# Score pieces moved from the middle to the end of a step's second product

## The chip, the cores and the metric

One core of one Trainium2 chip runs the whole program in one launch. The metric is device time in microseconds (us), the median of several runs. TensorE (PE) multiplies, with its weight loads listed apart (PEld); VectorE (DVE), ScalarE (ACT) and GpSimd (POOL) work on tiles; SyncE (SP) issues most DMAs.

## The reference, cut to what matters

Three layers follow one another: block-causal attention, a token-mixing layer with a two-layer perceptron, and a gated layer.

```python
scores = q @ k.T / 8, block-causal mask with blocks of 64   # 8 batches x 8 heads, 576 tokens, 64 wide
x      = softmax(scores) @ v                                # heads side by side: [8, 576, 512]
u      = x + (x.T @ U @ V).T                                # mixing over the tokens, rank 32
y      = u + relu(u @ w_ch1) @ w_ch2                        # 512 -> 2048 -> 512
out    = (sigmoid(causal_conv5(y)) * (y @ w_val)) @ w_out
```

## The kernel before, in words

**Perceptron.** The 4608 tokens are cut into 9 groups of 512 (`groups`). Each group is worked in 16 steps, one per 128 hidden units. A step has two products of 12 matmuls of 512 columns each. The first (`emit_h1`, L1000, matmuls at L987) sums a bank `h` of PSUM; ACT then writes `hh = relu(h)` (L1015) and DVE writes the rest `hl = max(h,0) - hh` (L1016), since every float32 product is made of three products of high and low parts. The second (`emit_o`, L1023, matmuls at L1036) adds `hh` and `hl` of the step before (`LAG = 1`) into four banks `acc` that are held over the group. So PE's row of work is h(s), o(s-1), h(s+1), o(s), and so on.

**Gaps.** PE runs in the order in which the program is written (`manual_schedule`). The order on the other engines is made by a scheduler when the program is built. Attention for later batches is a generator (`attention`, `tick`, L860) that is resumed in the gaps of the perceptron: `gap(0)` after six matmuls of the first product, `gap(1)` behind it, once ACT's and DVE's reads of the bank are issued, `gap(2)` after six matmuls of the second product, `gap(3)` behind it. These numbers are the kinds of a gap. A group has 64 gaps.

**The timetable.** From the tenth pair of heads on (`PAIR0`), each piece of attention waits in `until` (L844) for its gap. `begun[g]` is the count of gaps when group g began; pair i of the group gets its piece `what` at the first gap whose count is at least `begun[g] + POS0 + period * i + PLACES[..][what]`. The period is 12 gaps (three steps) in group 1, which takes five pairs, and 16 gaps (four steps) in groups 2 to 6, which take four, four, four, four and one. Pieces that put matmuls on PE also refuse a gap that another such piece has used. Only this line has a condition on the kind of gap:

```python
yield from until(n, f"S{i}", (2, 3))     # L876, i = 0 or 2
emit_s_piece(n // 2, i)
emit_s_piece(n // 2, i + 1)
```

**The pieces of a pair.** S0 and S1 together, then S2 and S3 together: scores of two heads (L420, two banks of PSUM a piece, one per head, copied out by ACT at L425). In between and behind: corner masks (POOL), block maxima (DVE L618), transposes of the next q and k (L398, L399), the running maximum of a head and its subtraction (DVE L651 to L671, `x` in the table for the odd head), the exponentials (ACT L687, in two halves of 832 and 768 columns) and sums (POOL L694, L696, DVE L703). V is probability times value (L729, L739, copied by ACT L741, divided by DVE L746 to L749 and POOL L750), T transposes (L789, L797), G and H mix over tokens (L805 with ACT L807, DVE L808; L828 with DVE L830). H of the batch's last pair ends the batch, and H pieces that had to wait for a free `u` buffer are put in at the group's end (`flush_later`).

**PSUM.** While attention runs, four banks are `acc` and four (`ps_p`, tag `a`) are shared by h, S, V, T, G and H in turn: a new piece takes the bank that was taken four allocations ago and waits until its reader, ACT or DVE, is done. S0, S1 take four in a row: the fourth is that of the piece before S0.

Of the kernel before, what the change touches and what calls it, by code (L numbers as in the profile page):

```python
# [22 lines left out]
def attn_moe_gate_kernel(ctx: ExitStack, tc: tile.TileContext, q, k, v, U, V, w1, w2, wval, convw, wout, out):  # L23
    nc = tc.nc
    B, H, S, D = q.shape
# [58 lines left out]
    FLUSH = 4  # L84
    PAIR0 = (NQ + EARLY) // 2
    PAIR1 = 3 * NP + 3
    POS0 = 6
    PLACES = (
        (12, {"S0": 0, "m0": 2, "S2": 4, "H0": 5, "H1": 6, "T0": 7, "T1": 8, "V": 9, "m1": 10, "G": 11, "x": 11}),
        (16, {"S0": 0, "m0": 2, "S2": 4, "H0": 5, "H1": 6, "T0": 7, "T1": 8, "V": 9, "m1": 11, "G": 14, "x": 15}),  # L90
# [254 lines left out]
    def load_v(n):  # L345
        if not 0 <= n < NH:
            return
        vv = v[n // H, n % H]
        t = vpart(n)
        sp.dma_start(out=t[:, 0:NK - 1, :], in_=vv[0:S - D, :].rearrange("(i p) d -> p i d", p=P))  # L350
        sp.dma_start(out=t[D:P, NK - 1, :], in_=vv[S - D:S, :])
# [56 lines left out]
    def emit_s_piece(pn, i):  # L408

        heads = (2 * pn, 2 * pn + 1)  # L410
        tq, tk = qkt[pn]
        if i == 0:
            for n in heads:
                stt[n] = [spare(("za", "zb")[h], w) if n % 3 == 1 else s_p.tile([P, w], F32, tag=f"s{h}", name=f"s{h}") for h, w in enumerate(sw)]
        ps = [psum["a"].tile([P, 512], F32, tag="a", name="pS") for _ in own]
        o = 0
        for j, a0, a1 in pieces[i]:
            w = a1 - a0
            for t, me in zip(ps, own):
                pe.matmul(t[:, o:o + w], tk[me, kslice(j)], tq[me, a0:a1], start=True, stop=True)  # L420
            o += w
        j, a0, a1 = pieces[i][0]
        d = soff[j] + a0 - q0[j]
        for n, t in zip(heads, ps):
            act.copy(stt[n][half_of[j]][:, d:d + o], t[:, 0:o])  # L425
# [172 lines left out]
    def emit_corners(n):  # L598
        for h, js in enumerate(((3, 0), (1, 2))):
            c0, c1 = (soff[j] // D for j in js)  # L600
            v_ = stt[n][h].rearrange("p (c w) -> p c w", w=D)
            pool.memset(v_[D:P, c0:c1 + 1:c1 - c0, :], MASKED)
        pool.memset(sv(n, NK - 1)[0:D], MASKED)
# [11 lines left out]
    def emit_max_a(n):  # L615
        r = tiny_p.tile([P, sum(nblk)], F32, tag="rb", name="rb")
        for half, (o, w) in enumerate(((0, nblk[0]), (nblk[0], nblk[1]))):
            x = vec.tensor_reduce(  # L618
                r[:, o:o + w],
                stt[n][half].rearrange("p (b a) -> p b a", a=BL),  # L620
                axis=AX.X,
                op=ALU.max,
                apply_transpose=True,
            )
        noted(1, x)
        mxt[n] = r

    def emit_max_b(n):

        t = mxt.pop(n)  # L630
        r = tiny_p.tile([P, NB32], F32, tag="r0", name="r0")

        def join(out, i, j):
            a, b = t[:, rblk[i]], t[:, rblk[j]]
            skip = (q0[j] - q0[i]) // BL
            if out is None:
                vec.tensor_tensor(a[:, skip:], a[:, skip:], b, op=ALU.max)
            else:
                vec.tensor_tensor(out[:, skip:], a[:, skip:], b, op=ALU.max)
                vec.tensor_copy(out[:, 0:skip], a[:, 0:skip])  # L640

        join(None, 1, 2)
        join(None, 3, 4)
        join(None, 1, 3)
        join(r, 0, 1)
        mxt[n] = r
# [21 lines left out]
    def emit_sub(n, half):  # L668
        mb = mbt[n]
        for j in parts[half]:  # L670
            noted(3, vec.tensor_tensor(sv(n, j), sv(n, j), mb[:, q0[j]:], op=ALU.subtract))  # L671
# [6 lines left out]
    def emit_exp(n):  # L678
        pn, a = divmod(n, 2)
        src = stt.pop(n)  # L680
        if a:
            dst = src
        else:
            e = late["e"] if pn % 2 and "e" in late else e_p
            dst = [e.tile([P, w], F32, tag=f"e{h}", name="e") for h, w in enumerate(sw)]
        for s, t in zip(src, dst):
            act.activation(t, s, AF.Exp, scale=scale)  # L687
        est[n] = dst
# [10 lines left out]
    def emit_sum_b(n):  # L699
        m = sums[n]  # L700
        r = tiny_p.tile([P, NB32], F32, tag="rs", bufs=3, name="rs")
        for o, t in ((slice(0, P // BL), ev(n, 0)[:, 0:P]), (slice(P // BL, NB32), m)):
            vec.tensor_reduce(r[:, o], t.rearrange("p (b a) -> p b a", a=BL), axis=AX.X, op=ALU.add, apply_transpose=True)  # L703
        sums[n] = r
# [12 lines left out]
    def emit_pv(pn, c):  # L717
        heads = (2 * pn, 2 * pn + 1)
        if c == 0:
            xts[pn] = (late["x"] if heads[0] >= 3 * H and pn % (NP + 2) == 0 else x_p).tile([P, S], F32, tag="xt", name="xt")  # L720
        xt = xts[pn]
        last[0] = (own[0], xt[own[0]][0:1, 0:1])
        ps = ps_p.tile([P, 512], F32, tag="a", name="pPV")
        c0, c1 = vbanks[c]
        js = [j for j in range(NK) if q0[j] < c1]
        for j in js:
            a0 = max(c0, q0[j])
            for n, me in zip(heads, own):
                pe.matmul(  # L729
                    ps[me, a0 - c0:c1 - c0],  # L730
                    vpart(n)[:, j, :],
                    est[n][half_of[j]][:, soff[j] + a0 - q0[j]:soff[j] + c1 - q0[j]],
                    start=j == 0,
                    stop=j == js[-1],
                )
        if c:
            f = ps[:, c1 - c0:c1 - c0 + NB32]
            for n, me in zip(heads, own):
                pe.matmul(f[me], quad, sums.pop(n), start=True, stop=True)  # L739
        with tc.high_priority():  # L740
            act.copy(xt[:, c0:c1], ps[:, 0:c1 - c0])  # L741
        if c:
            for n in heads:
                est.pop(n)
            r = tiny_p.tile([P, NB32], F32, tag="r0", name="r0")
            vec.tensor_scalar(r, f, 1e-9, None, op0=ALU.add)  # L746
            vec.reciprocal(r, r)
            rb = rot("t")
            vec.transpose(rb.rearrange("p (j a) -> p j a", a=32), r.rearrange("p (j o) -> p j o", o=1).to_broadcast([P, NB32, 32]))  # L749
            pool.tensor_tensor(xt, xt, rb, op=ALU.mult)  # L750
# [93 lines left out]
    def until(n, what, kinds=None):  # L844

        p = n // 2
        if p < PAIR0:
            return
        g, i = (1, p - PAIR0) if p < PAIR1 else (2 + (p - PAIR1) // NP, (p - PAIR1) % NP)
        period, place = PLACES[g > 1]  # L850
        busy = what[0] in "SHTVG"
        while at_gap["kind"] != FLUSH:
            c = at_gap["count"]
            if g in begun and c >= begun[g] + POS0 + period * i + place[what] and (kinds is None or at_gap["kind"] in kinds) and not (busy and at_gap["used"] == c):
                break
            yield WAITS
        if busy:
            at_gap["used"] = at_gap["count"]

    def tick(n, mixed, last=B * NP):  # L860


        e = n - DEPTH
        new, half = n < NH, n % 2
        pn = n // 2 - 1
        old = NQ <= 2 * pn < NH

        if old and not half:
            load_v(n - 2)
            load_v(n - 1)  # L870
        for i in range(4):
            if new and not half:
                if n < 2 * PAIR0:
                    emit_s_piece(n // 2, i)
                elif i % 2 == 0:
                    yield from until(n, f"S{i}", (2, 3))  # L876
                    emit_s_piece(n // 2, i)
                    emit_s_piece(n // 2, i + 1)
            if old and half and i == 0:
                yield from until(n, "V")  # L880
                emit_pv(pn, 0)
                emit_pv(pn, 1)
            if i == (0 if half else 3) and new:
                emit_corners(n)
                emit_max_a(n)
            if i == (2 if half or n < 2 * PAIR0 else 1) and NQ <= n - 1 < NH:
                yield from until(n, f"m{half}")
                emit_sum_b(n - 1)
            yield
        if new:  # L890
            emit_max_b(n)
            if half:
                prep_t((n + 1) // 2)
        yield from mixing(2 * e, mixed, last)
        if half:
            yield from until(n, "x")
        if new:
            for _ in emit_max_c(n):
                pass
            emit_sub(n, 0)  # L900
            emit_sub(n, 1)
            emit_exp(n)
            emit_sum_a(n)
        yield from mixing(2 * e + 1, mixed, last)
# [323 lines left out]
    for s in range(NS + LAG):  # L1228
        g, f = divmod(s, NF)
# [89 lines left out]
```

## Time and profile before

| | us |
|---|---|
| median of 3 runs | 1389.25 (1387.07 to 1389.58) |
| the profiled execution | 1385.46 |
| its span, first to last instruction | 1383.7 |
| PE busy | 1333.4 (96%) |
| DVE busy | 986.6 (71%) |
| ACT busy | 552.6 (40%) |
| POOL busy | 445.1 (32%) |
| mean granted clock of TensorE | 0.991 of full speed |

A matmul that follows another is listed with its whole length, 0.39 us for 512 columns, though one begins every 0.23 us. So the listed idle time of PE is less than what a wait costs: that is read from the start of the work behind the wait. Starts are counted from the start of the span.

### The profile page before, as it was taken

Reading aid. Unit: us, or ns where it says so; the run is one execution under the profiler, and the core shown is the slowest. Engines: PE = TensorE matmul, PEld = TensorE weight load, DVE = VectorE, ACT = ScalarE, POOL = GpSimd, SP = SyncE. Lnnn points to the kernel's source line nnn. Section 1 sums busy time; section 2 is a strip of 40 time slices with the busy share of each in tenths; the row PEclk is TensorE's granted clock in tenths of the full one; section 3 lists DMA queues with packets and bytes.
Section 4 is the critical chain, followed back from the end, with each engine's and each line's share of the span. In section 5 each row is a group of like instructions: output and inputs, shape, how many; then the busy total and the mean of one; then the engine's idle time right before and its main releaser. Section 6 shows DMA issues by size and latency. Waiting matters only on the chain.

```text
span 1383.7 us, 20054 instructions
## 1 busy us (share of the span) xinstructions
PE 1333.4 (96%) x6840; PEld 1029.5 (74%) x6840; DVE 986.6 (71%) x2085; ACT 552.6 (40%) x1210; POOL 445.1 (32%) x648
## 2 busy tenths in 40 slices
PE   6889889999999999999999999999999999999999
PEld 4667665777677777777777777778878888788887
DVE  5986789788878778777877877772235164699981
ACT  5785544333343334334433433432223122434432
POOL 3443334423343224334322422441132100624210
PEclk9999998999999999999999999999999999999999
DMA  6667785644364347435443644332375632332311
GB/s 109 159 179 209 230 263 170 140 95 115 78 135 107 93 113 155 111 92 142 104 99 96 155 105 111 102 103 88 116 206 167 154 128 99 77 107 77 107 60 62
DMA packets 257936, 173.60 MB, mean 125 GB/s; under 512 B 202149, under 2 KB 222885, under 8 KB 257834
## 3 DMA queue, kind: packets, MB, share of 16 engines
q1 hardware_dynamic: 250282, 162.58, 42.5%
q0 software_dynamic: 5184, 9.44, 4.5%
q8 instruction: 54, 0.88, 0.3%
q10 hardware_dynamic: 2368, 0.30, 0.2%
q14 instruction: 48, 0.39, 0.1%
HBM read 135.57 MB, written 36.70 MB: 125 GB/s over the span
## 4 chain that ended last, share of the span: by engine, by line
PE 59%; DVE 24%; ACT 7%; DMA 5%; issue 3%; SPq 1%; POOL 0%; ACTq 0%; DVEq 0%; POOLq 0%
PE acc L1036 18%; PE h L987 18%; PE o L1150 7%; PE val L1126 7%; PE pS L420 4%; DMA raw<-in_moe_w_ch_dram 3%; DVE hl L1016 2%; DVE mb L664 2%; PE pPV L729 2%; DVE s L671 2%; DVE r L657 2%; ACT e L687 1%; DVE wa L133 1%; DVE g L105 1%; ACT s L687 1%
## 5 line engine op out<-in xcount | busy, mean ns | idle before, releaser
L1036 PE MATMUL acc<-hh,w 128*128 128x512 f32 x1152 | 404.3, 404 | 1.6 <-DMA w<-w_s 1.6
L1036 PEld LDWEIGHTS acc<-hh,w 128*128 128x128 f32 x1152 | 218.2, 189 | 72.1 <-issue 23.4
L987 PE MATMUL h<-uh,w1hi 128*128 128x512 f32 x576 | 233.1, 405 | 1.2 <-DVE xt L830 1.0
L1036 PE MATMUL acc<-hl,w 128*128 128x512 f32 x576 | 226.7, 394 | 0.2 <-DVE hl L1016 0.2
L987 PE MATMUL h<-uh,w1lo 128*128 128x512 f32 x576 | 226.0, 392 | 0.0
L987 PE MATMUL h<-ul,w1hi 128*128 128x512 f32 x576 | 225.6, 392 | 0.0
L1016 DVE SCALAR_TENSOR_TENSOR hl<-h,hh 128x512 fp32r<-128x512 f32 x144 | 98.6, 685 | 141.3 <-ACT hh L1015 139.7
L1015 ACT ACTIVATE hh<-h 128x512 fp32r<-128x512 f32 x144 | 85.9, 597 | 242.2 <-PE h L987 241.8
L987 PEld LDWEIGHTS h<-uh,w1hi 128*128 128x128 f32 x576 | 108.8, 189 | 27.6 <-issue 1.8
L987 PEld LDWEIGHTS h<-uh,w1lo 128*128 128x128 f32 x576 | 108.7, 189 | 23.7
L1036 PEld LDWEIGHTS acc<-hl,w 128*128 128x128 f32 x576 | 109.5, 190 | 19.8 <-DVE hl L1016 0.5
L987 PEld LDWEIGHTS h<-ul,w1hi 128*128 128x128 f32 x576 | 109.0, 189 | 20.1 <-issue 0.4
L1108 DVE SCALAR_TENSOR_TENSOR gt<-yb,cw,gt 128x516 f32<-128x516 f32 (+1 forms) x144 | 115.2, 830 | 1.4
L420 PE MATMUL pS<-tq,tk 64*128 64x320 f32 (+4 forms) x576 | 99.0, 420 | 13.1 <-DVE hl L1016 10.2
L105 POOL TENSOR_TENSOR yl<-yb,yh 128x512 fp32r<-128x512 f32 (+7 forms) x64 | 66.8, 1077 | 102.7 <-ACT yh L99 102.6
L105 POOL TENSOR_TENSOR ul<-xt,uh 128x512 fp32r<-128x512 f32 (+7 forms) x64 | 60.2, 948 | 112.7 <-ACT uh L99 112.6
L420 PEld LDWEIGHTS pS<-tq,tk 64*128 64x128 f32 x576 | 52.2, 187 | 51.3 <-issue 24.6
L425 ACT COPY s<-pS 128x320 f32<-128x320 f32 (+2 forms) x128 | 59.6, 501 | 36.5 <-PE pS L420 36.5
L671 DVE TENSOR_TENSOR s<-s,mb 128x64 f32<-128x64 f32 (+4 forms) x160 | 70.6, 507 | 0.5
L694 POOL TENSOR_TENSOR m<-e 128x448 f32<-128x448 f32 x24 | 31.0, 1293 | 122.5 <-ACT e L687 117.7
L729 PE MATMUL pPV<-e,vstk 128*64 128x192 f32 (+4 forms) x384 | 70.2, 336 | 0.1
L729 PEld LDWEIGHTS pPV<-e,vstk 128*64 128x64 f32 x384 | 46.8, 137 | 24.5 <-issue 12.6
(180 smaller groups left out, 2502.9 us busy)
## 6 DMA issues: line engine op xcount, KB each, us to landing
w<-w_s SPq DMA_DIRECT2D x144, 512.0 KB, 3.5
rawq<-in_q_dram SPq DMA_DIRECT2D x128, 72.0 KB, 3.0
out_dram<-ot SPq DMA_DIRECT2D x35, 256.0 KB, 2.0
rawk<-in_k_dram SPq DMA_DIRECT2D x124, 72.0 KB, 2.9
vstk<-in_v_dram SPq DMA_DIRECT2D x68, 128.0 KB, 2.9
raw<-in_moe_w_ch_dram SPq DMA_DIRECT2D x64, 128.0 KB, 2.4
raw<-in_moe_w_ch_dram SPq DMA_DIRECT2D x16, 512.0 KB, 3.9
w_s<-wo SPq DMA_DIRECT2D x16, 512.0 KB, 4.3
```

The lines of the kernel that those rows point to most:

```text
L105: eng.tensor_tensor(o, i, f32(h), op=ALU.subtract)
L420: pe.matmul(t[:, o:o + w], tk[me, kslice(j)], tq[me, a0:a1], start=True, stop=True)
L425: act.copy(stt[n][half_of[j]][:, d:d + o], t[:, 0:o])
L671: noted(3, vec.tensor_tensor(sv(n, j), sv(n, j), mb[:, q0[j]:], op=ALU.subtract))
L729: pe.matmul(ps[me, a0 - c0:c1 - c0], vpart(n)[:, j, :], est[n][half_of[j]][:, soff[j] + a0 - q0[j]:soff[j] + c1 - q0[j]], start=j == 0, st ...
L987: pe.matmul(ps[:, 0:n], w[:, d, fs], x[:, d, 0:n], start=(d == 0 and i == 0), stop=(d == ND - 1 and i == 2))
L1015: act.activation(hh[:, 0:n], ps[:, 0:n], AF.Relu)
L1016: latest[0] = vec.scalar_tensor_tensor(hl[:, 0:n], ps[:, 0:n], 0.0, f32(hh[:, 0:n]), op0=ALU.max, op1=ALU.subtract)
L1036: pe.matmul(acc[d][:, 0:n], w[:, wi, ds], x[:, 0:n], start=(f == 0 and i == 0), stop=(f == NF - 1 and i == 2))
L1108: vec.scalar_tensor_tensor(gt[d][:, 0:gw], y[:, d, j:j + gw], cw[:, d, j:j + 1], gt[d][:, 0:gw], op0=ALU.mult, op1=ALU.add)
L1126: pe.matmul(ps[:, 0:n], w[:, d, es], x[:, d, 0:n], start=(i == 0), stop=(i == 3 * ND - 1))
L1150: pe.matmul(ps[:m, cs], x[:, e, a:a + m], w[:, e, cs], start=(i == 0), stop=(i == 3 * ND - 1))
```

## The change

`POS0`, the first gap of a group's first pair, goes from 6 to 8, and the score pieces take gaps of kind 3 alone, the end of the second product, instead of 2 or 3. Nothing else is changed; the instructions are the same.

```diff
-    POS0 = 6
+    POS0 = 8
...
-                    yield from until(n, f"S{i}", (2, 3))
+                    yield from until(n, f"S{i}", (3,))
```

PE, the second pair of group 4 (`acc` is the second product, `h` the first). Before:

```order
L1036 MATMUL acc_6870<-hh,w_7109 128x512
L1036 MATMUL acc_6870<-hl,w_7109 128x512
L1036 MATMUL acc_6870<-hh,w_7109 128x512
L420 MATMUL pS<-tq,tk 128x64 x2
L420 MATMUL pS<-tq,tk 128x192 x2
L420 MATMUL pS<-tq,tk 128x256 x2
L420 MATMUL pS<-tq,tk 128x320 x2
L1036 MATMUL acc_6871<-hh,w_7109 128x512
L1036 MATMUL acc_6871<-hl,w_7109 128x512
```

and with the change:

```order
L1036 MATMUL acc_6847<-hh,w_7086 128x512
L1036 MATMUL acc_6847<-hl,w_7086 128x512
L1036 MATMUL acc_6847<-hh,w_7086 128x512
L420 MATMUL pS<-tq,tk 128x64 x2
L420 MATMUL pS<-tq,tk 128x192 x2
L420 MATMUL pS<-tq,tk 128x256 x2
L420 MATMUL pS<-tq,tk 128x320 x2
L987 MATMUL h_7211<-uh,w1hi 128x512
L987 MATMUL h_7211<-ul,w1hi 128x512
```

S0 and S1 stood with six matmuls of the second product behind them, which need none of the four banks; now a first product stands there, which needs one. S2 and S3 move in the same way. T, V, G and H move by one or two gaps.

PE, the end of group 3 (H of the batch's last pair, and H pieces that had waited). Before:

```order
L987 MATMUL h_6621<-uh,w1hi 128x512
L987 MATMUL h_6621<-ul,w1hi 128x512
L987 MATMUL h_6621<-uh,w1lo 128x512
L828 MATMUL pH<-vst,g 128x320 x2
L1036 MATMUL acc_5603<-hh,w_6577 128x512
```

and with the change:

```order
L987 MATMUL h_6615<-uh,w1hi 128x512
L987 MATMUL h_6615<-ul,w1hi 128x512
L987 MATMUL h_6615<-uh,w1lo 128x512
L828 MATMUL pH<-vst,g 128x320 x3
L1036 MATMUL acc_5578<-hh,w_6577 128x512
```

Three H pieces now stand in one gap behind a first product, where two did; the ends of groups 1, 2, 4, 5 and 6 read alike with other widths. Between the last S2 of a group and the V that the next group begins with stood 60 matmuls of the two products, and now 54.

ACT, the first pair of group 4. Before:

```order
L807 COPY t<-pG 128x128
L99 CAST g<-t 128x128
L425 COPY za<-pS 128x512
L425 COPY s_6881<-pS 128x512
L425 COPY za<-pS 128x320
L687 ACTIVATE s_6533<-s_6533 128x832
L425 COPY s_6881<-pS 128x320
L687 ACTIVATE s_6534<-s_6534 128x768
```

and with the change:

```order
L807 COPY t<-pG 128x128
L99 CAST g<-t 128x128
L687 ACTIVATE s_6539<-s_6539 128x832
L425 COPY za<-pS 128x512
L425 COPY s_6887<-pS 128x512
L687 ACTIVATE s_6540<-s_6540 128x768
L425 COPY za<-pS 128x320
L425 COPY s_6887<-pS 128x320
```

The exponential of the odd head of the pair before now stands ahead of the first copy of S0. It is so at the first pair of groups 2 to 6. In group 1 it stands there in the third, fourth and fifth pair, before the change and with it.

## Rows read from the trace of the kernel before

**Rows 1.** Waits of PE over the whole span: total us, times, longest.
```profile
PE pS L420 <- DVE hl L1016: 10.2, 16, 2.1
```
**Rows 2.** Timeline of PE, S0 and S1 without a wait (start, us, engine, line).
```profile
658.87 1.79 PE L420 MATMUL pS<-tq,tk 64*128 64x64 f32 x16
660.59 0.50 PE L1036 MATMUL acc<-hh,w 128*128 128x512 f32 x1
```
**Rows 3.** Timeline of PE, S0 and S1 with a wait.
```profile
750.93 1.78 PE L420 MATMUL pS<-tq,tk 64*128 64x64 f32 x14
753.01 0.80 PE L420 MATMUL pS<-tq,tk 64*128 64x320 f32 x2 [0.30 <-DVE hl L1016]
753.74 0.50 PE L1036 MATMUL acc<-hh,w 128*128 128x512 f32 x1
```
**Rows 4.** Timeline of PE, S2 and S3 of the same pair.
```profile
759.41 1.56 PE L420 MATMUL pS<-tq,tk 64*128 64x448 f32 x8
760.90 0.50 PE L1036 MATMUL acc<-hh,w 128*128 128x512 f32 x1
```
**Rows 5.** Timeline of DVE and ACT around that wait.
```profile
752.26 0.69 DVE L1016 SCALAR_TENSOR_TENSOR hl<-h,hh 128x512 fp32r<-128x512 f32 x1
...
749.03 0.90 ACT L687 ACTIVATE s<-s 128x832 f32<-128x832 f32 x1 [4.75 <-DVE s L671]
...
751.10 0.59 ACT L1015 ACTIVATE hh<-h 128x512 fp32r<-128x512 f32 x1
752.21 0.59 ACT L425 COPY za<-pS 128x512 f32<-128x512 f32 x1 [0.52 <-PE pS L420]
...
760.46 0.53 ACT L425 COPY zb<-pS 128x448 f32<-128x448 f32 x1 [1.65 <-PE pS L420]
```
**Rows 6.** Stretches from an S2 to a later S2 (us, engines' busy us, clock, DMA).
```profile
274.61:387.63 113.02, 106.58 (x572) 78.11 (x571) 92.97 (x220) 42.26 (x87) 36.47 (x63) 0.97 0.39 93
387.63:418.19 30.56, 30.56 (x172) 23.60 (x171) 23.43 (x60) 14.59 (x31) 14.18 (x22) 1.00 0.68 152
...
883.25:914.35 31.10, 30.96 (x173) 23.85 (x172) 25.10 (x60) 15.35 (x31) 15.70 (x22) 1.00 0.58 144
418.19:511.81 93.62, 92.39 (x502) 70.25 (x501) 73.94 (x170) 34.14 (x69) 28.74 (x51) 1.00 0.40 102
...
790.12:883.25 93.13, 92.27 (x503) 70.15 (x502) 72.28 (x170) 33.45 (x69) 27.50 (x51) 1.00 0.41 99
```
**Rows 7.** Timeline of PE, DVE and ACT from group 3's end to group 4's first S0.
```profile
635.60 1.56 PE L420 MATMUL pS<-tq,tk 64*128 64x448 f32 x8
...
638.60 1.80 DVE L618 TRANSPOSE_TENSOR_REDUCE rb<-s 128x24 f32<-128x768 f32 x2
...
641.80 0.49 DVE L830 TENSOR_TENSOR xt<-pH,xt 128x320 f32<-128x320 f32 x1 [0.62 <-PE pH L828]
...
655.96 0.18 DVE L746 TENSOR_SCALAR r<-pPV 128x18 f32<-128x18 f32 x1 [0.55 <-ACT xt L741]
...
662.22 0.90 ACT L687 ACTIVATE s<-s 128x832 f32<-128x832 f32 x1 [0.66 <-DVE s L671]
```
**Rows 8.** Timeline of ACT and PE in group 1, fourth pair.
```profile
352.70 0.90 ACT L687 ACTIVATE za<-za 128x832 f32<-128x832 f32 x1 [3.74 <-DVE za L671]
...
358.45 2.29 PE L420 MATMUL pS<-tq,tk 64*128 64x448 f32 x8
360.67 0.50 PE L1036 MATMUL acc<-hh,w 128*128 128x512 f32 x1
```
**Rows 9.** Stretches in group 1 around waits (columns as in Rows 6; clock third from last).
```profile
297.00:300.00 3.00, 3.00 (x9) 2.34 (x9) 2.17 (x5) 0.00 (x0) 2.64 (x8) 0.57 0.00 0
320.00:324.00 4.00, 2.55 (x18) 1.62 (x17) 3.87 (x9) 0.80 (x2) 2.13 (x3) 1.00 0.00 0
382.00:385.00 3.00, 3.00 (x8) 2.43 (x8) 1.63 (x4) 1.81 (x4) 2.31 (x6) 0.51 0.51 175
```

## The prediction

> **What bounds the kernel now.** The list of waits names one thing in the stretch that the change touches: matmuls of score pieces wait for DVE's `hl`, 16 times, 10.2 us of listed idle time [rows 1]. The timeline shows what such a wait costs. Without one, the work behind S0 and S1 begins 660.59 - 658.87 = 1.72 us after S0 [rows 2]. With one that is listed as 0.30 it begins 753.74 - 750.93 = 2.81 us after it [rows 3]: 1.09 us, 0.79 more than listed. At 0.79 more for each, the 16 waits cost 10.2 + 12.6 = 22.8 us: twelve in groups 2 to 5 (all pairs but a group's first; 12 x 1.09 = 13.1) and four in group 1 (9.7). The wait is one for a bank. S0 and S1 take four banks in a row, and the fourth is that of the first product before them. Its `hl` ends at 752.95, and S1 goes on at 753.01, 0.06 later [rows 3, 5]. `hl` is late because ACT writes `hh` at 751.10, behind the exponentials that begin at 749.03 after 4.75 us of waiting for DVE's subtraction [rows 5]. So the loop that sets the period of 31.1 us (four stretches of three periods, 93.62 to 93.13, 373.1 in all [rows 6]) runs from S2 through DVE's long chain (maxima, subtraction), ACT's exponential and `hl` back to S1, and through 24 products to the next S2: 759.41 - 753.74 = 5.67 [rows 3, 4]. PE alone would need 1.09 less.
>
> **Inside a group (groups 2 to 5).** The change removes this wait: with six more products ahead of S0, `hl` of 752.95 would come before S1 needs it. It adds another: the first product that now follows S1 takes the bank of S0's first head, which ACT's copy frees. That copy runs from 1.28 to 1.87 us after S0's start (752.21 + 0.59 - 750.93 [rows 3, 5]); with the 0.06 the product begins at 1.93, not 1.72: 0.21 lost. Behind S2 and S3 the copy ends at 760.46 + 0.53 - 759.41 = 1.58, so 1.64 for 1.49 [rows 4, 5]: 0.15 lost. These waits were covered by six products of the second product, which need no bank; that cover is gone. I take 0.36 a pair, since the copies start as soon as PE is through. The bounds are 0 (a copy of 0.59 hidden) and 0.9 (an exponential of 0.90 [rows 5] in front of it). Sum: 12 x (0.36 - 1.09) = **-8.8**.
>
> **From group to group.** From the last S2 of one group to the first S2 of the next there are five stretches, 30.56 to 31.10, mean 30.7 [rows 6], with no wait for `hl`. Here the change adds two.
>
> First, three H pieces in one gap. They take three banks, and the third is that of the first product that has just ended. Counted from S2 at 635.60 [rows 7]: the product starts at 1.64, has 12 matmuls (2.73) and one H piece (0.15) in it, and ends near 4.6. DVE is through with the maxima at 638.60 + 1.80, that is 4.80, then has three additions of about 0.45 (0.49 listed [rows 7], 0.4 from start to start), then `hl`, 0.69 [rows 5]: 6.9. So the third H goes at 6.95 for 4.9: 2.05 lost. Before, the second product stood between.
>
> Second, the exponential of 832 columns that now stands ahead of S0's first copy on ACT. It hung on DVE's chain, which at a group's start hangs on V: DVE's step behind V begins at 655.96 (20.36 after S2), the exponential at 662.22, 6.26 later [rows 7]. V has 54 matmuls ahead instead of 60, which is 6 x 0.23 = 1.36 earlier, but is pushed by 0.15 and 2.05: 0.84 later, so 21.2. The exponential starts at 27.46 and ends at 28.36; the copy ends about 0.5 later, since ACT begins a row some 0.1 before the last one ends: 28.86. The first product follows at 28.92, the next S2 5.67 later at 34.6. Against 30.7 that is 3.9 a stretch. Were the copy on time, S0 at 25.4 and the product at 27.4 would give 33.0, 2.35 lost. I take 3.9, because each piece of it has its row; the bounds are 0.4 (the copies alone) and 4.7 (DVE's chain another 0.8 longer, as much as the rest of POOL's and DVE's rows here differ). Sum: 5 x 3.9 = **+19.5**.
>
> **Group 1.** Four intervals, 113.0 us [rows 6]. In its third to fifth pair the exponential stands ahead of the copy already, at 352.70 in the fourth [rows 8], but six products covered it. Now 352.70 + 0.90 + 0.5 + 0.06 + 5.67 = 359.8 would be the next S2, not 358.45 [rows 8]: 1.4 later. In exchange S2 and S3 lose their own wait (360.67 - 358.45 = 2.22, against 1.49: 0.73 [rows 4, 8]), and DVE's chain starts 0.7 earlier. That is +0.7 three times. The second pair, with the longest wait (2.1 listed, so 2.9), keeps its first copy ahead of the exponential and gains about 3. Sum: +2.1 - 3.1 = **-1.0**, with 3 either way.
>
> **The end.** Group 6 ends with three H pieces too, when DVE has less to do: `hh` 0.59, `hl` 0.69 [rows 5] and the steps between, 1.6; with the last S2's 0.15 it is **+1.7**. The DMAs keep their bytes; on SP's queue the weights of the second product now stand ahead of the q and k loads of their step instead of between them, so they come no later. m0, m1 and x make no PE work, and only place DVE's.
>
> **The sum.** -8.8 + 19.5 - 1.0 + 1.7 = +11.4. Against the profiled execution's 1385.46 that is 1396.9. The runs' median is 3.8 higher, so the forecast is 1389.25 + 11.4 = **1400.6 us**. A difference under 0.2% (2.8 us) is what a measurement of this kernel can't tell from none.
>
> **The rivals.**
>
> *Faster: the group starts are not late.* If DVE's chain at a group's start is through 1.6 us earlier than I have it (the exponential at 25.9 or before), S0's copy is on time; and if `hl` comes before DVE's additions, the third H waits 0.5. Then a stretch between groups loses 0.9, the pairs gain as above, group 1 gains 3: -8.8 + 4.5 - 3 + 0.7 = -6.6, 1382.6. For it: the 12 waits inside the groups do go, and DVE is busy only 23.43 of 30.56 us there [rows 6], so it has slack. Against it: ACT and DVE work in the order that the program has, and that order has the exponential ahead of the copy and the third addition behind `hl`. It decides at a loss of 1.6 a stretch, where 5 x 1.6 meets the gain.
>
> *No change.* Only one of the two comes, 2.35 a stretch, with group 1 gaining 3: -8.8 + 11.8 - 3 + 1.7 = +1.7, 1391.
>
> *Slower still: the clock.* Two of group 1's waits are followed by a clock of 0.57 and 0.51 of full (near the lower level of 1.2 GHz) for about 3 us [rows 9], which costs some 1.5 us each; a wait as long at 320 to 324 left it at 1.00. The change makes new waits of 1.5 to 4 us: one and a half to two at each of six group ends or starts, and three in group 1. If every one dropped the clock, 13 drops for two would cost 11 x 1.5 = 16 more: 1417. The Trainium skill ("TensorE: Matmul & The Clock Gate", section "What's actually happening") says that half clock is the default state and activity releases it, so that idle time brings it back; by that rule alone each long wait pays twice. The trace agrees in two waits of four.
>
> **How the numbers follow.** The forecast has 0.55 (its own range 1391 to 1410: the stretches between groups at 2.4 to 4.7, the copies inside at up to 0.6), the clock 0.13, no change 0.13, faster 0.19. So slower 0.68, same 0.13, faster 0.19. The range of 1383 to 1413 leaves out about half of the faster case and half of the clock's.
>
> **What would show it.** In the profile of the changed kernel: S1's waits for `hl` in groups 2 to 5 gone, and the first product behind S1 waiting for ACT's copy, 0.2 inside a group and 3 or so at its first pair; S2 to S2 at 30.4 inside groups, 34 to 35 across them; H waiting for `hl` at six group ends. It is wrong if stretches across groups stay below 32.3, or if those inside stay at 31.

## The result and the profile after

| | us |
|---|---|
| the kernel before, median of 4 runs | 1388.16 (1385.96 to 1389.58) |
| the changed kernel, median of 4 runs | 1400.37 (1399.16 to 1402.92) |
| ratio, with its 95% interval | 1.0092 (1.0071 to 1.0113) |
| the profiled execution, and its span | 1402.92, 1401.1 |
| mean granted clock of TensorE | 0.985 of full speed |

The changed kernel is slower by 12.2 us; the forecast was 11.4. The total came out, but three of its four terms didn't. Between the two profiled executions the span grew by 17.4 us, since the one of after is the slowest of its four runs and that of before was among the faster. Some of it stands already where both kernels still have the same instructions in the same order: `hh` of step 16 begins here at 264.47 in the kernel before and at 267.76 in the changed one. That 3.3 us is scatter between executions.

ACT of the kernel before, the first step of group 1 (start, us, engine, line):

```profile
264.47 0.62 ACT L1015 ACTIVATE hh<-h 128x512 fp32r<-128x512 f32 x1
```

and of the changed kernel:

```profile
267.76 0.62 ACT L1015 ACTIVATE hh<-h 128x512 fp32r<-128x512 f32 x1
```

**Where PE waits now.** The list of PE's waits of the changed kernel, over the whole span (total us, times, longest). Three of its rows carry the argument; all three are waits of the perceptron's first product:

```profile
PE h L987 <- ACT s L425: 12.3, 7, 2.8
...
PE h L987 <- DVE hl L1016: 6.8, 1, 6.8
...
PE h L987 <- ACT za L425: 4.4, 2, 2.8
```

The 16 waits of S1 for `hl` [rows 1] are gone. In their place first products wait for ACT's copies, as forecast. But one wait of 6.8 us is new, and it stands in no part of my prediction.

**The ledger.** Stretches of the changed kernel from an S2 to a later one (columns as in [rows 6]): group 1; the first and the last of the five from group to group; three periods inside group 2, and inside group 5:

```profile
279.58:396.52 116.94, 108.07 (x572) 80.03 (x571) 94.14 (x219) 42.91 (x87) 36.43 (x63) 0.94 0.34 90
396.52:429.33 32.81, 30.86 (x172) 23.68 (x171) 24.29 (x60) 14.25 (x31) 15.30 (x24) 1.00 0.64 142
892.07:925.94 33.87, 31.14 (x172) 23.77 (x172) 26.03 (x60) 15.27 (x31) 16.90 (x24) 1.00 0.54 132
429.33:520.43 91.10, 90.48 (x502) 69.39 (x501) 70.75 (x168) 33.44 (x69) 27.66 (x48) 1.00 0.38 105
801.11:892.07 90.96, 90.34 (x503) 69.31 (x502) 69.71 (x168) 33.21 (x69) 26.42 (x48) 1.00 0.37 101
```

| part | before | after | moved by | forecast |
|---|---|---|---|---|
| to the first S2 of group 1 | 274.61 | 279.58 | +5.0 | 0 |
| group 1, four intervals | 113.02 | 116.94 | +3.9 | -1.0 |
| inside groups 2 to 5, twelve periods | 373.1 | 363.9 | -9.2 | -8.8 |
| across groups, five stretches | 153.6 | 165.5 | +11.9 | +19.5 |
| from the last S2 to the end | 469.3 | 475.2 | +5.9 | +1.7 |

S2 itself stands six matmuls later in its step, 6 x 0.23 = 1.4 us: that part of the first row is no lost time, and the last row is too small by as much. The first row is then 3.3 of scatter and 0.3 of the change, and the last is 7.3.

**Inside a group** the reader sees the forecast, word for word. PE of the changed kernel, the third pair of group 4:

```profile
729.94 1.79 PE L420 MATMUL pS<-tq,tk 64*128 64x64 f32 x16
731.86 0.50 PE L987 MATMUL h<-uh,w1hi 128*128 128x512 f32 x1
...
737.54 1.56 PE L420 MATMUL pS<-tq,tk 64*128 64x448 f32 x8
739.18 0.50 PE L987 MATMUL h<-uh,w1hi 128*128 128x512 f32 x1
```

and ACT beside it:

```profile
731.22 1.73 ACT L425 COPY s<-pS 128x512 f32<-128x512 f32 x4 [0.43 <-PE pS L420]
```

The product follows S0 after 1.92 us and S2 after 1.64, for 1.93 and 1.64 in the prediction. The copy begins 1.28 after S0, as before the change.

**At a group's start** the late copy is there too. PE and ACT of the changed kernel, the first pair of group 4:

```profile
667.82 1.79 PE L420 MATMUL pS<-tq,tk 64*128 64x64 f32 x16
671.24 0.50 PE L987 MATMUL h<-uh,w1hi 128*128 128x512 f32 x1 [1.63 <-ACT za L425]
```

```profile
669.81 0.90 ACT L687 ACTIVATE s<-s 128x832 f32<-128x832 f32 x1 [2.50 <-DVE s L671]
670.62 0.57 ACT L425 COPY za<-pS 128x512 f32<-128x512 f32 x1
```

The copy stands behind the exponential and ends at 671.19; the product begins 3.42 behind S0 (3.5 forecast), five times.

**At a group's end** the wait that I forecast is not there. PE, its weight loads and DVE of the changed kernel, behind the last first product (`h`) of group 3:

```profile
648.78 0.93 PE L828 MATMUL pH<-vst,g 128*128 128x320 f32 x3
649.29 0.19 PEld L828 LDWEIGHTS pH<-vst,g 128*128 128x128 f32 x1 [0.32 <-DVE xt L830]
649.54 0.39 PE L1036 MATMUL acc<-hh,w 128*128 128x512 f32 x1
```

```profile
648.85 0.38 DVE L830 TENSOR_TENSOR xt<-pH,xt 128x256 f32<-128x256 f32 x1
...
650.10 0.68 DVE L1016 SCALAR_TENSOR_TENSOR hl<-h,hh 128x512 fp32r<-128x512 f32 x1
```

All three H pieces are through before 650, and `hl` of that product ends only at 650.78. So the third did not take the product's bank. It waited 0.3 for DVE's addition that ends at 649.23, that of the H piece in the middle of the product: the bank that comes free first. It is so at the ends of groups 1 to 5: the third H begins more than 1 us before that `hl` ends.

**Group 1.** ACT and PE of the changed kernel, fourth pair, and the stretch behind the wait:

```profile
356.86 0.90 ACT L687 ACTIVATE za<-za 128x832 f32<-128x832 f32 x1 [1.88 <-DVE za L671]
357.67 1.38 ACT L425 COPY s<-pS 128x512 f32<-128x512 f32 x3
```

```profile
352.85 2.66 PE L420 MATMUL pS<-tq,tk 64*128 64x64 f32 x16
358.29 0.50 PE L987 MATMUL h<-uh,w1hi 128*128 128x512 f32 x1 [2.78 <-ACT s L425]
```

```profile
360.00:363.00 3.00, 3.00 (x9) 2.35 (x8) 2.10 (x5) 0.37 (x2) 2.77 (x4) 0.50 0.00 0
```

The product begins 5.44 behind S0, in the third, fourth and fifth pair alike (5.43 in the third); with each of the three waits the granted clock falls (here to 0.50, the lower level of 1.2 GHz). From S0 to S2 it is 12.71 here; 5.44 + 5.67 = 11.1 would be the time without the lower clock, so that costs 1.6. In the fifth pair the clock stays at 0.50 from 387.0 to 393.6, twice as long, and S2 comes 13.65 behind S0: that costs 2.5.

**The new wait.** ACT of the changed kernel, `hh` of step 112, the casts and `hh` of step 113:

```profile
1015.70 0.60 ACT L1015 ACTIVATE hh<-h 128x512 fp32r<-128x512 f32 x1 [2.19 <-PE h L987]
1024.42 2.18 ACT L99 CAST yh<-yb 128x512 fp32r<-128x512 f32 x4 [8.13 <-DMA yb<-y_s]
1026.50 0.58 ACT L1015 ACTIVATE hh<-h 128x512 fp32r<-128x512 f32 x1
```

and of the kernel before, `hh` of step 114, the same casts and `hh` of step 115:

```profile
1015.99 0.57 ACT L1015 ACTIVATE hh<-h 128x512 fp32r<-128x512 f32 x1
1019.23 2.18 ACT L99 CAST yh<-yb 128x512 fp32r<-128x512 f32 x4 [2.67 <-DMA yb<-y_s]
1021.32 0.59 ACT L1015 ACTIVATE hh<-h 128x512 fp32r<-128x512 f32 x1
```

and PE and the clock of the changed kernel behind it:

```profile
1027.87 0.80 PE L987 MATMUL h<-uh,w1hi 128*128 128x512 f32 x1 [6.83 <-DVE hl L1016]
```

```profile
1027.80:1032.00 4.20, 4.13 (x10) 3.26 (x11) 4.06 (x6) 0.00 (x0) 2.47 (x2) 0.50 0.19 71
```

The four casts of the last layer's first input (`split_y`, L1095) stand in ACT's order two steps earlier than before, ahead of `hh` of step 113, and they wait 8.13 us for a load. `hh`, `hl` and the next product wait behind them, and PE goes on at half its clock. This is some 100 us behind the last score piece (S2 at 925.94), but not far behind attention's last H pieces, which the change did move: PE has three of them together at 1006.30 and one at 1009.73, where the kernel before has two, one and one, at 995.95, 999.17 and 1002.17.

The load itself stands elsewhere too. SP of the kernel before, the last write of an H piece's result and the load:

```profile
1003.32 0.32 SPq L831 DMA_DIRECT2D y_s<-xt  x1
1012.06 0.58 SPq L1088 DMA_DIRECT2D yb<-y_s  x1
```

and of the changed kernel:

```profile
1010.88 0.32 SPq L831 DMA_DIRECT2D y_s<-xt  x1
1012.02 0.59 SPq L1088 DMA_DIRECT2D yb<-y_s  x1
```

It is issued 1.1 us behind that write instead of 8.7, ahead of step 112's `hh` instead of behind step 113's, and takes 12.2 us instead of 7.1. That is no accident of one execution: in the profiles of E1 and of E3 to E7 below, with the changed kernel's order on SP, it takes 11.5 to 12.3, and in those of E2 and E8, with the old order there, 8.0 and 6.7. Why the scheduler put the casts and the load earlier no run shows.

### The profile page after: what moved, and what is told of

Its sections match the earlier page's. It is cut to its first block, busy times and chain, and to the rows that moved or that the text cites. A ratio compares the mean times of both kernels' runs of the same rounds, so it can differ in the third digit from the quotient of the medians.

```text
span 1401.1 us, 20058 instructions
## 1 busy us (share of the span) xinstructions
PE 1331.0 (95%) x6840; PEld 1030.2 (74%) x6840; DVE 981.2 (70%) x2085; ACT 549.4 (39%) x1210; POOL 443.6 (32%) x648
## 4 chain that ended last, share of the span: by engine, by line
PE 73%; DVE 14%; ACT 5%; DMA 5%; issue 2%; SPq 1%; ACTq 0%; DVEq 0%; POOL 0%
PE h L987 24%; PE acc L1036 22%; PE o L1150 7%; PE val L1126 7%; PE pPV L729 4%; PE pS L420 3%; DMA raw<-in_moe_w_ch_dram 2%; PE pS L459 2%; DVE rb L618 1%; ACT s L425 1%; DVE hl L1016 1%; DVE s L671 1%; ACT s L474 1%; DMA yb<-y_s 1%; DVE mb L664 1%
## 5 line engine op out<-in xcount | busy, mean ns | idle before, releaser
L1036 PE MATMUL acc<-hh,w 128*128 128x512 f32 x1152 | 391.9, 397 | 0.0
L987 PE MATMUL h<-uh,w1hi 128*128 128x512 f32 x576 | 241.6, 419 | 27.7 <-ACT s L425 12.3
L420 PE MATMUL pS<-tq,tk 64*128 64x320 f32 (+4 forms) x576 | 88.0, 417 | 4.8 <-ACT s L425 4.2
L105 POOL TENSOR_TENSOR ul<-xt,uh 128x512 fp32r<-128x512 f32 (+7 forms) x64 | 53.3, 846 | 117.2 <-ACT uh L99 116.9
L420 PEld LDWEIGHTS pS<-tq,tk 64*128 64x128 f32 x576 | 48.3, 187 | 36.0 <-issue 24.6
L618 DVE TRANSPOSE_TENSOR_REDUCE rb<-s 128x26 f32<-128x832 f32 (+1 forms) x64 | 61.4, 978 | 12.8 <-ACT s L425 9.6
```

The lines of the kernel that those rows point to most:

```text
L105: eng.tensor_tensor(o, i, f32(h), op=ALU.subtract)
L618: x = vec.tensor_reduce(r[:, o:o + w], stt[n][half].rearrange("p (b a) -> p b a", a=BL), axis=AX.X, op=ALU.max, apply_transpose=True,)
L987: pe.matmul(ps[:, 0:n], w[:, d, fs], x[:, d, 0:n], start=(d == 0 and i == 0), stop=(d == ND - 1 and i == 2))
L1036: pe.matmul(acc[d][:, 0:n], w[:, wi, ds], x[:, 0:n], start=(f == 0 and i == 0), stop=(f == NF - 1 and i == 2))
```

## The experiments

Each is timed against the kernel before on the same chip. In all of them the casts of `split_y(0, d)` are held back, so that none stands ahead of a `hh` of steps 112 to 115; the load keeps the place that the scheduler gives it:

```diff
                 if g_ == 0:
+                    vec.tensor_copy(gate[0][1][:, d, 0:1], hts[s][1][:, 0:1])
                     split_y(0, d)
```

(the column of `yh` that DVE writes is written over by the cast).

**E1, the changed kernel with that edit alone.**

> The changed kernel, but the four casts of the last layer's first input (yh from yb) are held until step 132 to 135 by a one-column write to yh that reads that step's hl; the order of all else stays. Theory A (the trace of the changed kernel): the cast that now stands ahead of hh in step 113 makes PE wait 6.83 us and is followed by 4.2 us at a clock of 0.50, 7.2 us in all between steps 112 and 116; without it the time is 12.2 - 7.2 = 5.0 us over the kernel before, 1393.2, and PE has no wait for hl behind step 112. Rival B (a transfer that happened to be late in one execution, or a wait that only moves to where the cast is now): as the change, 12 over, 1400.4.

1.0035 of the kernel before (1.0019 to 1.005), where the change has 1.0092 (1.0071 to 1.0113): 4.9 us over it, for 5.0 expected. PE's wait for `hl` behind step 112 is gone. So some 7 of the change's 12 us are those casts. In their place PE waits for weights of the second product, as it did in the kernel before. That row of the waits behind 960 us, of the kernel before and of E1:

```profile
PE acc L1036 <- DMA w<-w_s: 1.6, 1, 1.6
```

```profile
PE acc L1036 <- DMA w<-w_s: 2.5, 1, 2.5
```

From the first product of step 112 to that of step 116 it is 20.9 us in the kernel before, 28.1 with the change and 21.9 in E1: the place has a wait of its own, also without the casts.

**E2, the kernel before with the same edit.**

> The kernel before, with the casts held back in the same way. Theory A: in the kernel before the cast stood behind hh and cost nothing, so nothing changes: within 1.5 us of the kernel before, 1388.2. Rival B (the casts cost something wherever they are, or cost less when late): 2 us or more to either side.

0.9993 (0.9976 to 1.001): nothing, as expected of the order and not of the casts as such. In its profiled execution, one of its slower ones, the wait for the weights is 3.4 us, with the lower clock behind it, and these four steps take 25.2: so the place differs by 4 us between two executions in which no cast holds PE up.

**E3, group 1 on the old timetable.** (Both edits of the change undone for `g == 1`, in `until`, where `pos` then takes the place of `POS0`.)

```diff
+        pos = 6 if g == 1 else POS0
+        if kinds and g == 1:
+            kinds = (2, 3)
```

> The changed kernel with the casts held back, and with group 1 on the old timetable (POS0 6, score pieces in gaps of kind 2 or 3). Theory A: group 1's four intervals from S2 to S2 took 116.9 instead of 113.0 us, since three first products wait 5.4 us behind S0 for ACT's copy, with the lower clock behind them; that part, 4 us, goes: 1393.2 - 4.1 = 1389.1, 1 over the kernel before. Rival B (my forecast's size for group 1, -1.0): the time rises by 1 against the kernel with the casts alone, to 1394.

1.0018 (1.0006 to 1.003): 2.4 us less than E1. The two intervals overlap, so the time alone leaves it open; the traces say the same (group 1 takes 112.12 in E3 and 114.42 in E1, with the lower clock twice in each), so group 1 loses by the change and does not gain 1.0. It is less than the 4.1 expected from the two traces. The trace of E1 says why: group 1 takes 114.42 there, not 116.94. Stretches of E1, group 1 and then from S0 to S2 of its fourth and its fifth pair:

```profile
282.65:397.07 114.42, 105.58 (x572) 78.13 (x572) 94.11 (x219) 42.93 (x87) 36.41 (x63) 0.97 0.36 92
355.95:367.04 11.09, 8.25 (x41) 5.95 (x40) 9.68 (x21) 4.14 (x8) 5.00 (x11) 1.00 0.14 49
384.35:397.07 12.72, 9.88 (x41) 7.08 (x41) 9.67 (x21) 4.14 (x8) 4.99 (x11) 0.87 0.12 41
```

The two pairs wait alike, 5.42 behind S0. One is followed by the lower clock, the other by a clock of 1.00, and takes the 11.1 worked out above.

**E4, S0 of the first pair of groups 2 to 6 at its old gap.**

```diff
+        pos = POS0
+        if g > 1 and i == 0 and what == "S0":
+            pos, kinds = 6, (2, 3)
```

> The changed kernel with the casts held back, and with S0 of the first pair of groups 2 to 6 alone at its old gap (the middle of the second product, POS0 6). Theory A: the stretches across groups took 32.8 to 33.9 for 30.6 to 31.1 us, 11.9 in all, because the exponential stands ahead of S0's first copy and nothing lies between S1 and the product that waits for it; with the copy ahead again and six products behind S1 the stretches take about 31.0, so 5 x 1.9 = 9.5 less: 1383.7, 4.5 under the kernel before. Rival B (it is the H pieces or DVE's chain, not the order of copy and exponential, that makes the stretches long): 2 us less at most, 1391.

0.9977 (0.9961 to 0.9993): by the ratios 3.2 us under the kernel before, and 8 under E1. The five stretches take 31.12, 31.08, 31.09, 31.54 and 32.19, 8.5 less than with the change. It is the first S0 of a group that makes the starts late, not the H pieces. It moves two things at once, the order on ACT and the six products behind S1; the next experiment moves only the first.

**E5, S0's copies ahead of the exponential at the starts of groups 2 to 6, S0 where the change has it.**

```diff
+    held_exp = []
...
+                    if i == 0 and held_exp:
+                        m = held_exp.pop()
+                        s = stt[n][half_of[4]][0:1, soff[4]:soff[4] + 1]
+                        t = stt[m][0][0:1, 0:1]
+                        vec.scalar_tensor_tensor(t, s, 0.0, t, op0=ALU.mult, op1=ALU.add)
+                        emit_exp(m)
+                        emit_sum_a(m)
...
-            emit_exp(n)
-            emit_sum_a(n)
+            p = (n + 1) // 2
+            if half and (p >= PAIR1 and p < NH // 2 and (p - PAIR1) % NP == 0):
+                held_exp.append(n)
+            else:
+                emit_exp(n)
+                emit_sum_a(n)
```

> The changed kernel with the casts held back; besides, at the first pair of groups 2 to 6 ACT does S0's first two copies before the odd exponential (the exponential is issued behind S0, and one element of its input is rewritten by DVE from S0's copy times zero, so that it can't go ahead). The place of S0 stays. Theory A (the order of copy and exponential makes the starts late): the product behind S1 follows S0 after 1.95 us instead of 3.42, five times, 7.3 us less than with the casts alone: 1.0035 - 0.0053 = 0.998 of the kernel before. Rival B (the start is late because S0 has no six products behind it, whatever ACT does; or what the exponential loses is paid in the next V): less than 3 us of gain, 1.002 or more.

0.9996 (0.9978 to 1.0014), 5.4 us under E1 by the ratios, for 7.3 expected; the interval takes in the 0.998. ACT of E5, first pair of group 4, whose S0 begins at 662.54:

```profile
663.82 0.59 ACT L425 COPY za<-pS 128x512 f32<-128x512 f32 x1 [1.79 <-PE pS L420]
...
665.52 1.63 ACT L687 ACTIVATE s<-s 128x768 f32<-128x768 f32 x2 [0.63 <-DVE s L884]
```

The copy begins 1.28 behind S0, and the product 1.92 behind it at every one of the five starts (1.97 at two) instead of 3.42. The stretches across groups are 31.38, 31.32, 31.31, 31.78 and 32.44, 158.2 in all: 7.2 less than with the change. So the order of copy and exponential is the main cause of the late starts; what the place of S0 adds by itself is the difference to the 157.0 of E4, 1.2.

**E6, the same in group 1 as well** (the condition begins with `PAIR0 < p < PAIR1 or`).

> As the one before, and the same in group 1, from its second pair to its fifth. Theory A: the three first products that waited to 5.43 us behind S0 follow after 1.95; 3 x 3.5 = 10.5 less, and the lower clock behind two or three of these waits goes as well, 1.6 each, 3 to 5 more; against that the second copies of S1 come 0.9 later and DVE's maxima with them. Some 10 us less than the kernel with the copies first at the starts alone: 0.991 of the kernel before, which would beat both kernels. Rival B: in group 1 DVE's chain sets the period (S to S) and the gain comes back as another wait: 0 to 4 us less, 0.995 to 0.998.

0.994 (0.992 to 0.9961), 1380.82 us: 8 under E5, and faster than both kernels. It lies between the two expectations: 8 us where A has some 10 and B 0 to 4, though the ratio itself is nearer to B's 0.995 than to A's 0.991, since E5 had come out 0.0016 higher than expected. Group 1 of E6, from the first S2 to the fifth:

```profile
282.16:387.16 105.00, 104.00 (x572) 76.42 (x571) 92.97 (x220) 43.13 (x87) 34.49 (x60) 1.00 0.40 100
```

8.0 less than in the kernel before and 11.9 less than with the change, at a clock of 1.00. PE is busy 104.00 of the 105.00. The gain does come back in part as other waits: the list of waits of E6 has S2 waiting for `hl` four times, from the third pair on S0 is followed by the product after 2.70 to 2.75, not 1.95, and the stretch from group 1 to group 2 takes 32.4 for 31.4 in E5.

**E7, group 1 and each group's first S0 at the old places.** (E3 and E4 together.)

> The casts held back, group 1 on the old timetable, and the first S0 of groups 2 to 6 at its old gap: what is left of the change are the score pieces of the other pairs in groups 2 to 5 at the end of the second product. Theory A, where the parts add: 0.9977 of the kernel before with the first S0 alone, less the 2.4 us (0.0017) that group 1 gave: 0.996, 5.6 us under the kernel before; by the rows 12 x 0.73 = 8.8 gained inside the groups less 5 x 0.5 at the group ends. Rival B (the gains don't add, since a stretch that is shorter lets the next one wait): 0.998.

0.9967 (0.9953 to 0.9981), 4.6 us under the kernel before, for 5.6 expected. The interval takes in A's 0.996 and B's 0.998, so the time doesn't settle whether the parts add. The trace is as A has it: 30.3 to 30.4 a period inside the groups, as with the change, and from group 2 on the stretches across groups are within 0.04 of those of E4.

**E8, POS0 back to 6, score pieces at the end of the second product.**

> The casts held back, POS0 back to 6, and score pieces in gaps of kind 3 only. The score pieces stand in the same gaps as with the change; only G and the odd head's subtraction and exponential (x) are one or two gaps earlier inside the groups, and at the starts of groups all is in the same order. Theory A (the place of the score pieces does all of it, the later timetable of the other pieces nothing): as the change with the casts held, 1.0035, within 2 us. Rival B (the later timetable costs, by a later exponential): 4 us less or more, 1.000 or below.

1.006 (1.0039 to 1.0082); E1 had 1.0035 (1.0019 to 1.005). Whether it is slower than E1 these intervals don't settle, and A's 2 us are exceeded by 1.5 in the ratios; nothing shows it faster, so no gain by the earlier G and x is seen. One thing more differs: the last H pieces and the load at the end stand as in the kernel before. Its trace has the same kinds of wait: 3.41 at the starts, 5.26, 5.23 and 5.26 in group 1, and 4.22 for 2.45 in group 1's second pair. The other half, POS0 8 with the old condition (2, 3), gives the same order of instructions on every engine as the change: at POS0 8 the first gap of kind 2 or 3 is one of kind 3. So the edit of POS0 alone makes the change, and the edit of the condition adds nothing to it.

## Why the prediction was right, and where it was not

*The time and its sign* came out (1400.6 against 1400.37), but by errors that cancel: across groups it was 7.6 too high, in group 1 4.9 too low, and at the end 5.6 too low. That the total fits is luck, and no confirmation of the sum.

*Inside a group* every step held: the wait for `hl` goes, the copies add 0.2 and 0.15, twelve periods give 9.2 for 8.8.

*From group to group*, two mechanisms were forecast. The exponential ahead of the copy is right, shown by E5, with its size (3.42 for 3.5). The step that failed is "They take three banks, and the third is that of the first product that has just ended", 2.05 us a stretch: the third H took the bank that came free first. I had carried the rule of four in turn, as the section on PSUM has it, over from S0 and S1. There it can't be told from this one, since S0 and S1 fill four banks, and any rule leaves the product's bank as the last. Without the 2.05 the forecast of 3.9 is 1.85; measured are 2.1 to 2.8, 2.4 in the mean. What is left has two waits beside it that the kernel before doesn't have, seen at the weight loads: the third H's, 0.2 to 0.4, and V's for `x`, 0.4 in three stretches, 0.9 and 1.4 in the last two. The same step gave the +1.7 at the end of group 6, which is not there.

*Group 1.* The late copies were forecast with their size: three products 5.43 to 5.44 behind S0, where the rows gave 5.65, and 3.9 before the change: 1.5 each for 1.4. The step that failed is the "exchange" against them. Of the second pair I took 3 off, and its S0 is followed 2.1 sooner (2.45 for 4.58). Of S2's wait I took 0.7 off three times: it came off twice, 0.6 each, while in the second pair S2 was followed 0.9 later and in the fifth 0.15. By waits that is 4.5 - 2.1 - 1.2 + 1.05 = +2.3 for my -1.0, and E3 against E1 measured 2.4. The other 1.6 of the profiled 3.9 lies in the 24 products from there to S2, 28.4 in the four pairs for 26.8: the lower clock comes three times for two, once twice as long (8.2 in that pair, 7.25 in the other two, 5.67 without it). Against that, the same row took 6.06 and not 5.67 in the third and fourth pair of the kernel before: the six products had not covered the late copy there altogether.

*The end.* No step of the prediction looked at the orders of ACT and SP behind the last H pieces. ACT's differs there by the place of four casts, two steps of 144, and that is worth some 7 us (E1, E2); SP's by that of the load before them. Both stood in the program and could have been seen.

*The rival of the clock* had 0.13. From group 1 on lower clocks came four times in the changed kernel, three in group 1 and one at the end, for two before; behind the waits of 1.6 listed at the group starts there was none (clock 1.00 in these stretches). The rule of the Trainium skill ("TensorE: Matmul & The Clock Gate", section "What's actually happening"), that idle time brings the throttled state back, held behind 6.8 us and behind waits of 2.8 in three cases of three here, and in three of three in E4, but in E1 and E5 in two of three alike waits: by these runs a wait of that length makes the lower clock likely, not certain.

## What to carry to other kernels

Cover counts on both sides of a move: S1's wait went when six products came ahead of it, and a new one came where six products no longer stood behind it. Where one in-order engine frees a buffer that the bound engine needs, look at what stands ahead of the freeing copy; here two copies ahead of one exponential, at five group starts and in group 1, took the changed kernel with its casts held back from 1.0035 to 0.994 (E1, E6). And compare the order of every engine to the end of the program, not only around the edit: here casts that hang on a load slipped ahead of the bound engine's supply, 100 us behind the last piece that the edit names.

## What I had not expected

At the group ends the bank was not taken in turn but as it came free (0.3 us of wait instead of 2.05). The load that the casts hung on was issued two steps earlier in the changed kernel and took 12.2 us instead of 7.1: of 10.3 us that it was issued earlier, counted from `hh` of step 112 (1005.41 before, 1015.70 with the change), half was lost again. And the same wait, 5.42 us from S0 to the product, costs 1.6 more or nothing, as the lower clock follows it or not: so two executions of one kernel can differ by that much at such a wait.
